# Moving 24 weight buffers by 64 bytes within each partition of on-chip memory: a spectral mix and two feed-forward layers on one core

## The chip, the cores and the metric

The kernel runs on one core of a Trainium2 chip. The metric is the device time of one execution in microseconds (us), taken as the median of several runs. A second number, the span, comes from one profiled execution: it runs from the first to the last instruction that the hardware profiler recorded.

## What is computed

The input is `x` of shape (4, 3072, 256). Three layers follow one another. The first is a Fourier transform along the sequence, a complex 256x256 product with `w_r` and `w_i`, a bias and a soft threshold, and the inverse transform. The second and third are:

```python
h = x @ w_in                               # (tokens, 256) @ (256, 2048): the first product
g = h * tanh(softplus(h))
x = g @ w_out                              # (tokens, 2048) @ (2048, 256): the second product

x_prev = x shifted by one token
xk = mu_k * x + (1 - mu_k) * x_prev
xr = mu_r * x + (1 - mu_r) * x_prev
k = relu(xk @ w_k)                         # 256 -> 1024
v = k * k @ w_v                            # 1024 -> 256
out = sigmoid(xr @ w_r2) * v               # w_r2 is moe2_w_r, 256 -> 256
```

All arrays are float32, and the three layers see 12288 tokens.

## The kernel before

**Precision.** A product in `part2` splits each operand into a high part `hi` (rounded to `F32R`, a float32 that TensorE takes in one pass) and the rest `lo`, and sums three matmuls: `wh*hi`, `wh*lo`, `wl*hi`. `mm(o, l, r, ...)` (L154) makes one MATMUL out of `r`, the operand that streams through the array (the moving one), with `l`, the operand that an LDWEIGHTS puts into the array first (the stationary one). Every MATMUL has its own LDWEIGHTS.

**Part 1** makes the transforms. `emit_F` multiplies lines of `a` (stationary) by the forward constants `fm` (moving), `emit_M` multiplies `xh`, `xl` (stationary) by the mixing weights `wmh`, `wml` (moving), and `emit_I` multiplies `yb` (stationary) by the inverse constants `im` (moving). `fm`, `im`, `a` and `yb` are plain float32.

**Part 2** takes the tokens in 24 blocks `j` of 512 and the hidden columns of the second layer in 16 chunks `c` of 128, so that a step `s` is a pair (j, c). Each step issues on TensorE, in this order: `emit_H(s)` (6 matmuls of 512 columns, tile `hps`), then whatever the table `PLAN` puts there of `emit_K` (6 of 512 columns, `kps`), `emit_V` (12 of 256 columns, `v`) and `emit_R` (12 of 256 columns, `zps`) for the third layer, and at last `emit_acc(s - 3)` (6 of 512 columns, `a`), the second product. ScalarE and VectorE turn `hps` into `gh`, `gl` and `kps` into `kh`, `kl` meanwhile.

**Where operands lie.** Pools take their place in a partition one behind the other, in the order in which they are opened. The small constants and `cst` end at byte 16576 of a partition, which is 192 modulo 256. Every tile from there on is a multiple of 256 bytes long, so that every operand begins at 192 modulo 256. One exception is there already: in `part2` a pool of 64 bytes stands ahead of `kk` (L819), so that `ka`, `kh`, `kl` and the tile `r` of pool `sg` begin at 0 modulo 256.

```python
            xk_p = pool(es, "xk", 1)
            pool(es, "gap", 1).tile([128, 16], F32, name="gap")
            kk_p = pool(es, "kk", 2)
```

The pool `mat` has 24 buffers of 2 KB. In part 1 they hold `fm` and `im`; later they are written again with `wo`, the weights of the second product (16 tiles, `wout_piece`, L487), and with `wkt`, the tiles of `w_k` (8 tiles, `fetch`, L510). The places of the operands of each product, modulo 256:

| product | rows named | stationary | moving | columns |
|---|---|---|---|---|
| first | hps<-yh,win / yl,win | `win` 192 | `yh`, `yl` 192 | 512 |
| second | a<-gh,wo / gl,wo | `wo` 192 | `gh`, `gl` 192 | 512 |
| w_k | kps<-xkh,wkt / xkl,wkt / b,wkt | `wkt` 192 | `xk` 192 | 512 |
| w_v | v<-b,kh / b,kl | `kh`, `kl` **0** | `wt["v"]` in `b` 192 | 256 |
| w_r2 | zps<-b | `xr` in `b` 192 | `wt["g"]` in `b` 192 | 256 |
| F, I (part 1) | xps<-fm,a / bps<-im,yb | `a`, `yb` 192 | `fm`, `im` 192 | 256 |
| mix (part 1) | yps<-wmh,xh and the like | `xh`, `xl` 192 | `wmh`, `wml` 192 | 512 |

Of the kernel before, what the change touches and what calls it, by code (L numbers as in the profile page):

```python
# [10 lines left out]
F32 = mybir.dt.float32  # L11
# [102 lines left out]
def tile_fft_mix_moe_channel_mix(  # L114
# [23 lines left out]
    def pool(stack, name, bufs, **kw):  # L138
        return stack.enter_context(tc.tile_pool(name=name, bufs=bufs, reuse_waits="tile", **kw))
# [21 lines left out]

    cst = pool(ctx, "cst", 1)
    big = pool(ctx, "big", 2)
    mat = pool(ctx, "mat", 24)
    g_p = pool(ctx, "g", 1)
    y_p = pool(ctx, "y", 1)
    yhl_p = pool(ctx, "yhl", 2)
# [900 lines left out]
```

## Time and profile before

| | |
|---|---|
| median of 3 runs | 1985.57 us (1985.16 to 1986.27) |
| the profiled execution, its own time | 1985.22 us |
| its span | 1983.2 us |
| PE (matmuls) busy | 1960.9 us, 10084 matmuls |
| PEld (weight loads) busy | 1687.4 us, 10084 loads |
| VectorE (DVE) / ScalarE (ACT) busy | 1143.1 us / 925.1 us |
| granted TensorE clock | 1.0 (the 2.4 GHz level) |

A matmul's duration in the profile is longer than the distance from its start to the next one's, since matmuls are pipelined. What counts for the time is the distance between starts.

### The profile page before, as it was taken

The page shows a single profiled execution, that of the slowest core. Times are in us where ns is not written, and L with a number is a line of the kernel's source. Part 1 is how long each engine was busy: PE and PEld are TensorE (multiplying, and loading weights), DVE is VectorE, ACT ScalarE, POOL GpSimd, SP SyncE. Part 2 cuts the span into 40 slices and gives each one's busy share as a digit, 9 for nine tenths or more (in the row PEclk, how much of TensorE's full clock was granted, in tenths as well). Part 3 has the DMA queues.
Part 4 walks back from the last instruction along what each step waited for, and adds up shares of the span by engine and source line. Part 5 has one row for each costly group of instructions (what it writes and reads, how often), then busy time and mean ns, then how long its engine had stood idle before and what let it go on. Part 6 is the DMA issues. An engine that isn't in the chain of part 4 may idle for free.

```text
span 1983.2 us, 25749 instructions
## 1 busy us (share of the span) xinstructions
PE 1960.9 (99%) x10084; PEld 1687.4 (85%) x10084; DVE 1143.1 (58%) x2183; ACT 925.1 (47%) x1525; POOL 13.5 (1%) x28
## 2 busy tenths in 40 slices
PE   6999999999999999999999999999999999999999
PEld 5888888888888888888888888888888888888888
DVE  8999986655654764465375445555444543444444
ACT  2423286344444544444444445444443544444455
POOL 0000000000000000000000000000000000000000
PEclk9999999999999999999999999999999999999999
DMA  9445276011011010101101001011000000000000
GB/s 278 151 136 170 71 246 202 34 33 64 22 33 54 22 46 9 54 22 33 54 22 54 1 22 54 8 31 38 22 1 22 22 11 11 22 22 1 22 11 22
DMA packets 104553, 106.66 MB, mean 54 GB/s; under 512 B 7016, under 2 KB 85488, under 8 KB 103408
## 3 DMA queue, kind: packets, MB, share of 16 engines
q1 hardware_dynamic: 104432, 105.02, 16.7%
q8 instruction: 79, 1.29, 0.3%
q14 instruction: 42, 0.34, 0.1%
HBM read 62.53 MB, written 42.47 MB: 53 GB/s over the span
## 4 chain that ended last, share of the span: by engine, by line
PE 97%; DMA 1%; DVE 1%; ACT 1%; issue 0%; SPq 0%; DVEq 0%; ACTq 0%
PE a L155 26%; PE hps L155 26%; PE v L155 14%; PE kps L155 13%; PE yps L155 7%; PE bps L155 4%; PE xps L155 4%; PE zps L155 3%; DMA a<-in_x_dram 0%; DMA w_dr<-wp 0%; DMA wraw<-in_w_r_dram 0%; DMA im<-in_inv_dram 0%; ACT sg L152 0%; SPq L266 0%; DVE q L149 0%
## 5 line engine op out<-in xcount | busy, mean ns | idle before, releaser
L864 DVE CAST gh<-u 128x512 fp32r<-128x512 f32 x384 | 163.4, 425 | 685.1 <-PE a L155 594.3
L155 PE MATMUL a<-gh,wo 128*128 128x512 f32 x1536 | 536.7, 390 | 0.0
L155 PE MATMUL hps<-yh,win 128*128 128x512 f32 x1536 | 534.7, 389 | 0.0
L152 ACT ACTIVATE u<-hps 128x512 f32<-128x512 f32 x384 | 229.7, 598 | 483.1 <-PE hps L155 428.5
L155 PEld LDWEIGHTS hps<-yh,win 128*128 128x128 f32 x1536 | 288.4, 188 | 60.4
L155 PEld LDWEIGHTS a<-gh,wo 128*128 128x128 f32 x1536 | 288.6, 188 | 57.8
L155 PE MATMUL a<-gl,wo 128*128 128x512 f32 x768 | 300.1, 391 | 0.0
L155 PE MATMUL hps<-yl,win 128*128 128x512 f32 x768 | 298.8, 389 | 0.0
L155 PE MATMUL v<-b,kh 128*128 128x256 f32 x1536 | 279.8, 281 | 0.0
L146 DVE TENSOR_TENSOR gl<-u,gh 128x512 fp32r<-128x512 f32 x384 | 263.9, 687 | 3.6
L155 PEld LDWEIGHTS v<-b,kh 128*128 128x128 f32 x1536 | 249.6, 189 | 14.3
L155 PE MATMUL v<-b,kl 128*128 128x256 f32 x768 | 215.8, 281 | 0.0
L152 ACT ACTIVATE ka<-kps 128x512 f32<-128x512 f32 x192 | 114.8, 598 | 211.0 <-PE kps L155 210.9
L155 PEld LDWEIGHTS hps<-yl,win 128*128 128x128 f32 x768 | 144.2, 188 | 29.8
L155 PEld LDWEIGHTS a<-gl,wo 128*128 128x128 f32 x768 | 144.7, 188 | 25.7
L146 DVE TENSOR_TENSOR kl<-ka,kh 128x512 fp32r<-128x512 f32 x192 | 132.9, 692 | 44.0 <-ACT ka L152 29.4
L155 PE MATMUL kps<-xkl,wkt 128*128 128x512 f32 x384 | 150.7, 392 | 0.0
L155 PEld LDWEIGHTS v<-b,kl 128*128 128x128 f32 x768 | 144.2, 188 | 0.0
L155 PE MATMUL kps<-b,wkt 128*128 128x512 f32 x384 | 134.5, 391 | 0.0
L155 PE MATMUL kps<-xkh,wkt 128*128 128x512 f32 x384 | 134.0, 391 | 0.0
L152 ACT ACTIVATE ka<-ka 128x512 f32<-128x512 f32 x192 | 121.8, 634 | 6.1
L152 ACT ACTIVATE kh<-ka 128x512 fp32r<-128x512 f32 x192 | 121.6, 633 | 6.1
(80 smaller groups left out, 2069.8 us busy)
## 6 DMA issues: line engine op xcount, KB each, us to landing
b_dr<-bs SPq DMA_DIRECT2D x48, 256.0 KB, 2.2
g<-b_dr SPq DMA_DIRECT2D x8, 1536.0 KB, 6.7
y<-y_dr SPq DMA_DIRECT2D x48, 256.0 KB, 3.1
out_dram<-r SPq DMA_DIRECT2D x48, 256.0 KB, 2.2
y_dr<-g SPq DMA_DIRECT2D x80, 64.0 KB, 1.7
w_dr<-wp SPq DMA_DIRECT2D x9, 512.0 KB, 5.8
a<-in_x_dram SPq DMA_DIRECT2D x8, 512.0 KB, 6.2
y_dr<-g SPq DMA_DIRECT2D x32, 128.0 KB, 1.9
```

The lines of the kernel that those rows point to most:

```text
L146: V.tensor_tensor(out=o, in0=a, in1=b, op=op)
L152: S.activation(out=o, in_=i, func=f, **kw)
L155: T.matmul(out=o, lhsT=l, rhs=r, start=start, stop=stop, **kw)
L864: return [lambda: V.tensor_copy(hi, u), lambda: tt(lo, u, hi.bitcast(F32), SUB)]
```

## The change

Two unused pools are opened around `mat`. The first is 64 bytes long and moves `mat` by 64 bytes; the second is 192 bytes long, so that everything behind it moves by 256 bytes in all and keeps its place modulo 256.

```diff
     cst = pool(ctx, "cst", 1)
     big = pool(ctx, "big", 2)
+
+    pool(ctx, "gap1", 1).tile([128, 16], F32, name="gap1")
     mat = pool(ctx, "mat", 24)
+    pool(ctx, "gap2", 1).tile([128, 48], F32, name="gap2")
     g_p = pool(ctx, "g", 1)
```

`fm`, `im`, `wo` and `wkt` now begin at 0 modulo 256; every other operand stays at 192, and `kk` and `sg` stay at 0. Each engine issues the same instructions in the same order as before.

## Rows read from the trace of the kernel before

**Rows 1.** The page: busy time of each engine, and the granted clock.

```profile
PE 1960.9 (99%) x10084; PEld 1687.4 (85%) x10084; DVE 1143.1 (58%) x2183; ACT 925.1 (47%) x1525; POOL 13.5 (1%) x28
...
PEclk9999999999999999999999999999999999999999
```

**Rows 2.** Waits of PE: all there are.

```profile
PE xps L155 <- DVE g L146: 17.6, 2, 16.2
PE yps L155 <- ACT zl L628: 0.5, 1, 0.5
PE bps L155 <- DVE yb L149: 0.2, 1, 0.2
```

**Rows 3.** Groups of instructions: matmuls by product (count, busy us, mean ns).

```profile
L155 PE MATMUL a<-gh,wo 128*128 128x512 f32 x1536 | 536.7, 390 | 0.0
L155 PE MATMUL hps<-yh,win 128*128 128x512 f32 x1536 | 534.7, 389 | 0.0
L155 PE MATMUL a<-gl,wo 128*128 128x512 f32 x768 | 300.1, 391 | 0.0
L155 PE MATMUL hps<-yl,win 128*128 128x512 f32 x768 | 298.8, 389 | 0.0
L155 PE MATMUL v<-b,kh 128*128 128x256 f32 x1536 | 279.8, 281 | 0.0
...
L155 PE MATMUL kps<-xkl,wkt 128*128 128x512 f32 x384 | 150.7, 392 | 0.0
...
L155 PE MATMUL kps<-b,wkt 128*128 128x512 f32 x384 | 134.5, 391 | 0.0
L155 PE MATMUL kps<-xkh,wkt 128*128 128x512 f32 x384 | 134.0, 391 | 0.0
...
L155 PE MATMUL bps<-im,yb 128*128 128x256 f32 x384 | 90.6, 379 | 0.2 <-DVE yb L149 0.2
...
L155 PE MATMUL xps<-fm,a 128*128 128x256 f32 (+1 forms) x352 | 80.6, 372 | 0.0
L155 PE MATMUL zps<-b 128*128 128x256 f32 x576 | 76.6, 283 | 0.0
```

**Rows 4.** Timeline of PE, an R group, then second product, H, V (start, us).

```profile
984.44 1.60 PE L155 MATMUL zps<-b 128*128 128x256 f32 x12
985.88 0.40 PE L155 MATMUL a<-gh,wo 128*128 128x512 f32 x1
...
987.26 0.39 PE L155 MATMUL hps<-yh,win 128*128 128x512 f32 x1
...
988.62 0.40 PE L155 MATMUL v<-b,kh 128*128 128x256 f32 x2
...
990.04 0.40 PE L155 MATMUL kps<-b,wkt 128*128 128x512 f32 x1
```

**Rows 5.** Timeline of PEld around the change from H to V.

```profile
1022.49 0.19 PEld L155 LDWEIGHTS hps<-yh,win 128*128 128x128 f32 x1
1022.72 0.41 PEld L155 LDWEIGHTS v<-b,kh 128*128 128x128 f32 x2
```

**Rows 6.** Groups at 1022.72 us: the last two matmuls of H ahead of V.

```profile
L155 PE MATMUL hps<-yl,win 128*128 128x512 f32 x1 | 0.4, 389 | 0.0
L155 PE MATMUL hps<-yh,win 128*128 128x512 f32 x1 | 0.4, 388 | 0.0
```

**Rows 7.** Groups at 984.22 us: the last two matmuls of H ahead of R.

```profile
L155 PE MATMUL hps<-yh,win 128*128 128x512 f32 x1 | 0.4, 389 | 0.0
```

**Rows 8.** Groups from 985.87 to 987.25 us: the second product behind an R group.

```profile
L155 PE MATMUL a<-gh,wo 128*128 128x512 f32 x4 | 1.4, 392 | 0.0
L155 PE MATMUL a<-gl,wo 128*128 128x512 f32 x2 | 0.8, 396 | 0.0
```

**Rows 9.** Timeline of PE in part 1: an I and an F group.

```profile
57.65 1.89 PE L155 MATMUL bps<-im,yb 128*128 128x256 f32 x8
59.37 1.89 PE L155 MATMUL xps<-fm,a 128*128 128x256 f32 x8
```

## The prediction

> **What bounds the kernel now.** I first read the busy shares and the clock: TensorE is busy for 99% of the span, and its granted clock stays at the upper level, 2.4 GHz [rows 1]. Then the waits: all waits of its matmuls come to 18.3 us, of which 17.6 are two waits of the first transforms for `g` [rows 2]. So nothing that another engine does sets the time; it is the sum of the distances between matmul starts. The third view is the groups by product [rows 3]. What a reader is to compare there is the mean duration of matmuls of one shape. A duration is not the distance between starts, but the two move together: 12 `zps` matmuls of 283 ns begin within 985.88 - 984.44 = 1.44 us, 120 ns apart, and 12 `v` matmuls of 281 ns within 990.04 - 988.62 = 1.42 us, 118 ns apart [rows 4]. Both times the duration is the distance plus 163 ns. So a mean in rows 3 that falls by 1 ns is 1 ns of span for each matmul.
>
> **What the change touches.** It neither adds nor removes an instruction, and no engine's order moves. What is new is one relation: for `a` (1536 + 768 matmuls) and `kps` (3 x 384), 3456 matmuls together [rows 3], the weights that are loaded begin at 0 modulo 256 while the operand that streams begins at 192. Before, both began at 192. The weights of one matmul are loaded while the one before it streams: the load for the first `v` begins at 1022.72, the start of the last `hps` [rows 5, 6]. So if the two reads get in each other's way, the place of one against the other could matter. Three comparisons within before bear on it.
>
> 1. *Matmuls of 256 columns, one behind the other.* `v` is the only product whose weights (`kh`, `kl`) lie at 0 while its moving operand lies at 192. `zps` has the same shape, the same high-high-low order, and both at 192. `v` takes 281 ns, `zps` 283 [rows 3]. If the place is the reason, it is worth 2 ns a matmul.
> 2. *One matmul of 512 columns with a shifted load under it.* The last `hps` ahead of a V group streams from 192 while weights at 0 are loaded: 388 ns [rows 6]. The last `hps` ahead of an R group has weights at 192 under it: 389 ns [rows 7]. All else about the two is alike. This is just the situation in which the change puts each `a` and `kps`, and it is worth 1 ns.
> 3. *Matmuls of 512 columns right behind 256-column groups.* They are slow whatever the place: after R, where everything lies at 192, the six of the second product take 4 x 392 + 2 x 396 = 2360 ns instead of 6 x 389 = 2334, 26 ns more [rows 8]. By the means, these slow groups cost 1536 x 1 + 768 x 2 (`a`) + 384 x 3 + 768 x 2 (`kps`) = 5.8 us in all against 389 [rows 3]. That `kps` and `a` are dearer than `hps` is thus a matter of what stands ahead of them, for rows of undisturbed groups are at 389 too. I leave these 5.8 us as they are; the bounds are that they go (-5.8) and that all groups become so (rival 3).
>
> **The sum.** A load at 0 comes under one matmul for each of the 3456, six for each group of six (the first under the last matmul of the group ahead). I take the 1 ns of comparison 2, since it has the same 512 columns and the same two places: 3456 x 1 ns = 3.5 us less. With the price of comparison 1 it is 3456 x 2 = 6.9 us less; these matmuls have 512 columns and those of comparison 1 have 256, so I take the nearer row and keep 6.9 as a bound. Durations are whole nanoseconds, so that the 1 ns itself may be anything from a half to one and a half: 1.7 to 5.2 us.
>
> The rest I cost at nothing:
> - *`fm` and `im` as moving operands.* `bps` and `xps` are float32 matmuls; eight `bps` records begin within 59.37 - 57.65 = 1.72 us, 215 ns apart [rows 9], for 256 columns, which is nearly double the 118 to 120 ns of `v` and `zps`. Columns are read half as fast, and no row here has the two operands at different places. With the 2 ns of comparison 1 in either direction, the 384 + 352 records [rows 3] are worth 1.5 us at most.
> - *Writes into `mat`* (loads of `fm`, `im`, `wkt`, and the decoding of `wo`) are work of DMA, ScalarE and VectorE, which TensorE does not wait for [rows 2]; if that cover were gone, those 17.6 us are the only place where it would show, and the tiles there (`g`, `a`) do not move modulo 256.
> - *Everything behind the second gap* moves by 256 bytes. `kps<-b` and `kps<-xkh` take 391 ns each [rows 3] though `b` begins at 69824 and `xkh` at 192960, which differ by 256 modulo 512: a shift by 256 bytes shows nothing.
>
> The profiled execution took 1985.22 us with a span of 1983.2; 3.5 less is 1981.7 and a span of 1979.7. The median of the runs stands 0.35 us higher, so the forecast for the median is 1985.57 - 3.5 = **1982.1 us**, 0.18% less. A measurement of this kernel can tell about 0.2%, 4.0 us, from no change, so that this counts as the same by a little.
>
> **The rivals.**
> 1. *The place does not matter at all* and the time stays at 1985.6. Then `v` differs from `zps` for another reason (other weights, another accumulator), and the 388 ns of rows 6 come from the kind of matmul that follows. Against it: the matmul ahead of `zps`, also of 256 columns, has 389 [rows 7]. For it speaks a rule. The Trainium skill says, on the page "TensorE: Matmul & The Clock Gate", section "Step-by-step: what each phase is for", that TensorE has two independent read ports, so that loading the next weights takes no read bandwidth from the running matmul; by that rule no place could change anything, and the sum would be 0. The 281 against 283 ns do not fit it, but they do not disprove it either.
> 2. *The dear end of the gain.* The steady pattern in which every load is shifted is worth what `v` shows: 2 ns on 3456, 1985.6 - 6.9 = 1978.7; if the slow groups of 26 ns go as well, another 5.8, 1972.9. For it: `v` is the only long run of shifted loads. Against it: in `v` loads and matmuls follow each other twice as densely.
> 3. *Slower.* The distance of a load from the stream decides, and 64 bytes can also bring the worse distance. Rows 8 show that the same two operands at the same places can cost 26 ns in six when they start in another rhythm, so the 389 ns is no ceiling. If the shift makes this the standing rhythm of `a` and `kps`, the groups that do not pay yet begin to: 3456 / 6 = 576 groups, of which 5.8 / 0.026 = 223 pay already, leaves 353 x 26 ns = 9.2 us, 1994.8. It decides from the point where a matmul with a shifted load under it stands above 389 ns inside a group and not only at its edge; rows 6 show one matmul at the edge, and nothing about the next. Half of it, if only one of the two products falls into that rhythm, is 1990.
>
> **How the numbers follow.** The forecast (1.7 to 5.2 us less) has 0.40, no effect 0.20, the larger gain 0.20, slower 0.17, and 0.03 is left for a much larger gain (the reads no longer meet at all). Faster by more than 0.2% are the larger gains and the upper quarter of the forecast: 0.2 + 0.03 + 0.10 = 0.33. Slower by more than 0.2% are rival 3 and a price of `fm` and `im` that comes on top of it or of no effect: 0.20. The rest, 0.47, is the same. The range takes in the 2 ns with half of the slow groups gone, 6.9 + 2.9 = 9.8 below (1975.8), and most of rival 3, 7.4 above (1993.0): outside lie the rest of rival 2 and the upper half of rival 3, less than 2 in 10. The forecast's own range is 1980.4 to 1983.9.
>
> **What would show it.** Right: in the groups by product, `a<-gh` goes from 390 to 389, `a<-gl` from 391 to 390, `kps` down by 1, while `hps`, `v` and `zps` keep 389, 281 and 283; an undisturbed `a` matmul stands at 388; `bps` keeps 379. Rival 1: all means stay. Rival 2: undisturbed `a` and `kps` at 387, or no step up behind `v` and `zps`. Rival 3: `a` and `kps` at 392 and above also where `hps` or `kps` stands ahead. The forecast is wrong in its reason if the time moves and these means do not, above all if `xps`, `bps` or a wait has moved instead.

## The result, and the profile after

The changed kernel takes 2004.85 us (median of 5 runs, 2004.69 to 2005.22) against 1985.57: a ratio of 1.0097 with a 95% interval of 1.0086 to 1.0108. It is 19.3 us slower, where 3.5 us less had been forecast, and it lies outside the range, whose upper end was 1993.0. The span of the profiled execution went from 1983.2 to 2002.7 us, 19.5 more.

The page of the changed kernel shows the same bound as before [rows 1]:

```profile
PE 1980.9 (99%) x10084; PEld 1682.8 (84%) x10084; DVE 1143.4 (57%) x2183; ACT 923.6 (46%) x1525; POOL 13.5 (1%) x28
...
PEclk9999999999999999999999999999999999999999
```

TensorE is busy 20.0 us longer, the loads are not (1687.4 to 1682.8), and the clock stays at the 2.4 GHz level. The waits of PE, in the order us, times, longest, do not grow either [rows 2]:

```profile
PE xps L155 <- DVE g L146: 17.0, 2, 15.6
PE bps L155 <- DVE yb L149: 0.3, 1, 0.3
PE yps L155 <- ACT zl L631: 0.3, 1, 0.3
```

So TensorE waits no longer than before, and it is matmuls themselves that take longer. The groups by product (count, busy us, mean ns) tell which [rows 3]:

```profile
L155 PE MATMUL a<-gh,wo 128*128 128x512 f32 x1536 | 544.4, 395 | 0.0
L155 PE MATMUL hps<-yh,win 128*128 128x512 f32 x1536 | 538.8, 392 | 0.0
L155 PE MATMUL a<-gl,wo 128*128 128x512 f32 x768 | 303.9, 396 | 0.0
L155 PE MATMUL hps<-yl,win 128*128 128x512 f32 x768 | 301.9, 393 | 0.0
L155 PE MATMUL v<-b,kh 128*128 128x256 f32 x1536 | 275.6, 279 | 0.0
L155 PE MATMUL v<-b,kl 128*128 128x256 f32 x768 | 213.6, 278 | 0.0
L155 PE MATMUL kps<-xkl,wkt 128*128 128x512 f32 x384 | 152.2, 396 | 0.1
L155 PE MATMUL kps<-b,wkt 128*128 128x512 f32 x384 | 136.0, 395 | 0.0
L155 PE MATMUL kps<-xkh,wkt 128*128 128x512 f32 x384 | 135.5, 395 | 0.0
L155 PE MATMUL bps<-im,yb 128*128 128x256 f32 x384 | 90.7, 379 | 0.4 <-DVE yb L149 0.3
L155 PE MATMUL xps<-fm,a 128*128 128x256 f32 (+1 forms) x352 | 80.6, 372 | 0.0
L155 PE MATMUL zps<-b 128*128 128x256 f32 x576 | 76.5, 283 | 0.0
```

Mean against mean: `a` 5 ns on 2304 matmuls is 11.5 us; `kps` 4 ns on 1152 is 4.6; `hps`, whose operands did not change their places, 3 ns on 1536 and 4 on 768, 7.7; `v`, unchanged as well, 2 ns less on 1536 and 3 less on 768 (281 before for both), -5.4. The sum is 18.4 of the 19.5 us; means are in whole nanoseconds. Part 1 with its `fm` and `im` did not move (379 and 372 as before), nor did `zps`. The line of `v<-b,kl` before, which [rows 3] leaves out:

```profile
L155 PE MATMUL v<-b,kl 128*128 128x256 f32 x768 | 215.8, 281 | 0.0
```

The timeline of PE shows the same in the groups of six and twelve. Each line is the first matmul of a group (start in us):

```profile
1002.49 0.39 PE L155 MATMUL kps<-b,wkt 128*128 128x512 f32 x1
...
1003.89 0.40 PE L155 MATMUL a<-gh,wo 128*128 128x512 f32 x1
...
1005.29 0.39 PE L155 MATMUL hps<-yh,win 128*128 128x512 f32 x1
...
1006.68 0.41 PE L155 MATMUL v<-b,kh 128*128 128x256 f32 x2
...
1008.06 0.39 PE L155 MATMUL a<-gh,wo 128*128 128x512 f32 x1
...
1009.46 0.39 PE L155 MATMUL hps<-yh,win 128*128 128x512 f32 x1
...
1010.83 0.40 PE L155 MATMUL a<-gh,wo 128*128 128x512 f32 x1
```

`kps` and `a` take 1.40 us each, `hps` behind them 1.39, and `v` 1.38. Before, six undisturbed matmuls took 1.36 us (from 987.26 to 988.62 in [rows 4]), and `v` 1.42. The `a` behind `v` also takes 1.40, but a group behind matmuls of 256 columns was slow already, 1.38 in [rows 4], and so grows by less; the `hps` behind it takes only 1.37.

### The profile page after: what moved, and what is told of

The parts are those of the page before. It is cut to its first block, busy times and chain, and to the rows that moved or that the text cites. A ratio compares the mean times of both kernels' runs of the same rounds, so it can differ in the third digit from the quotient of the medians.

```text
span 2002.7 us, 25749 instructions
## 1 busy us (share of the span) xinstructions
PE 1980.9 (99%) x10084; PEld 1682.8 (84%) x10084; DVE 1143.4 (57%) x2183; ACT 923.6 (46%) x1525; POOL 13.5 (1%) x28
## 4 chain that ended last, share of the span: by engine, by line
PE 94%; DVE 4%; DMA 1%; ACT 0%; SPq 0%; issue 0%; DVEq 0%
PE a L155 27%; PE hps L155 26%; PE kps L155 13%; PE v L155 13%; PE yps L155 5%; PE zps L155 3%; PE bps L155 3%; PE xps L155 3%; DVE a L146 1%; DVE a L149 1%; DVE yb L149 0%; DVE q L149 0%; DMA w_dr<-wp 0%; DVE xl L146 0%; DMA a<-in_x_dram 0%; DMA im<-in_inv_dram 0%
## 5 line engine op out<-in xcount | busy, mean ns | idle before, releaser
L155 PE MATMUL a<-gh,wo 128*128 128x512 f32 x1536 | 544.4, 395 | 0.0
L155 PE MATMUL v<-b,kh 128*128 128x256 f32 x1536 | 275.6, 279 | 0.0
```

Source lines behind the costliest of these rows:

```text
L155: T.matmul(out=o, lhsT=l, rhs=r, start=start, stop=stop, **kw)
```

## The experiments

Eleven kernels ran. They issue the same instructions in the same order; only places differ. Times are medians, each beside runs of the kernel before on the same chip (1985.6). "Place" is the place modulo 256. Streams begin at 192 unless they are moved: weights at 0 then lie 64 bytes behind them (at a higher address), weights at 128 lie 64 bytes ahead.

### Moving everything by 256 bytes (mat256)

```diff
+    pool(ctx, "gap1", 1).tile([128, 64], F32, name="gap1")
     mat = pool(ctx, "mat", 24)
```

> Everything from the pool mat on lies 256 bytes further, so that all places modulo 256 are those of the kernel before. Theory A (what costs is the relation of a load to the stream modulo 256): within 1.5 us of 1985.6, a and kps at 390 to 392 ns, hps 389. Theory B (what costs is that mat was moved at all, or its distance from big in bytes): 1995 to 2005, a at 395 ns and hps at 392.

Measured: 1985.48 us, ratio 1.0 (0.9989 to 1.0011), `a` at 390 and 391 ns, `hps` at 389, as before. Theory B falls: that `mat` moved, and that it lies 256 bytes further from `big`, costs nothing. What costs must be a place within 256 bytes.

### 128 bytes, and 64 bytes the other way (mat128, mat192)

```diff
+    pool(ctx, "gap1", 1).tile([128, 32], F32, name="gap1")
     mat = pool(ctx, "mat", 24)
+    pool(ctx, "gap2", 1).tile([128, 32], F32, name="gap2")
```

This is mat128; in mat192 the two are 48 and 16 floats long.

> mat lies 128 bytes off (64 modulo 256), the rest keeps its place modulo 256. Theory A: not the time of before, and not that of 64 bytes either: if the cost grows with the distance, 2010 to 2025 (a above 395 ns); if 64 bytes is a bad place and 128 is away from it, 1975 to 1995. Theory B: 2005 within 2 us, as with 64 bytes.

> The change with the other sign: wo and wkt at 128, 64 bytes ahead of the streams instead of 64 behind. Theory F without a sign (any mismatch throws the rhythm off): 1998 to 2008, undisturbed a groups near 1398 ns. If the sign decides also for 512 columns, as it did for what follows v (kk128): a groups at or under 1360 ns and 1978 to 1990.

Measured: 2005.93 us (1.0103, 1.0073 to 1.0132) with weights 128 bytes behind the streams, `a` at 395 and 396 ns; 1991.98 us (1.0034, 1.0023 to 1.0046) with weights 64 bytes ahead of them. For mat128 theory A missed on both sides, and the time is the one that theory B gave, which mat256 excludes. The total is near that of 64 bytes, but its parts are not the same: `a` pays as much, `hps<-yl` (390 ns) and `kps` (393 to 395) pay less, and `v` gives hardly anything back (280 and 281). For mat192 both cases missed the time. The sign matters, but for matmuls of 512 columns no distance tried (64 bytes either way, 128) beats none. Part of the 6.4 us of mat192 lies in part 1, whose `fm` and `im` moved too: its `yps` matmuls rose by 2 to 4 ns (from 429, 381 and 380 to 433, 383 and 382). In mat192 a `kps` group takes 1.38 us and an `a` group behind it 1.37 (timeline of PE):

```profile
997.85 0.39 PE L155 MATMUL kps<-b,wkt 128*128 128x512 f32 x1
...
999.23 0.39 PE L155 MATMUL a<-gh,wo 128*128 128x512 f32 x1
...
1000.60 0.39 PE L155 MATMUL hps<-yh,win 128*128 128x512 f32 x1
```

### One of the two products alone (wo_only, wk_only)

`mat` becomes two pools of 16 and 8 buffers; `wo` later lies in the one and `wkt` in the other, and only one of them is moved (shown for `wo`).

```diff
-    mat = pool(ctx, "mat", 24)
+    pool(ctx, "gapa", 1).tile([128, 16], F32, name="gapa")
+    mat = pool(ctx, "mat", 16)
+    pool(ctx, "gapb", 1).tile([128, 48], F32, name="gapb")
+    mk = pool(ctx, "mk", 8)
...
-                    fm[ORD[i]] = mat.tile([128, 2, 256], F32, tag="m", name="fm")
+                    fm[ORD[i]] = (mat if len(fm) + len(im) < 16 else mk).tile([128, 2, 256], F32, tag="m", name="fm")
...
-            wt["k", c] = mat.tile([128, 2, 2, 128], F32R, tag="m", name="wkt")
+            wt["k", c] = mk.tile([128, 2, 2, 128], F32R, tag="m", name="wkt")
```

> Two pools in place of mat, 16 buffers that later hold wo and 8 that later hold wkt; only the first pool lies 64 bytes off. Theory A: about two thirds of the 19.3 us, 1998 (1995 to 2001), kps behind H at 389 to 390 ns, and hps slow only behind a. If the loss came from kps or from fm and im alone: below 1990 or unchanged at 2005.

> Only the pool that holds wkt lies 64 bytes off. Theory F (a mismatched load throws the rhythm of loads and streams off, and the groups behind it need about five 512-column matmuls to come back): kps 1395 to 1400 ns a group also behind H (1360 before), and the second product behind it, whose operands match, 24 to 28 ns a group dearer; hps back at 389; 1993 to 1997. Theory A2 (only the mismatched matmuls pay): kps 4 to 6 us dearer in all, the second product unchanged, 1990 to 1992.

Measured: 2000.83 us for `wo` alone (1.0077, 1.0048 to 1.0106), 1994.73 for `wkt` alone (1.0046, 1.0030 to 1.0062), both inside what was expected (1995 to 2001, and 1993 to 1997 by theory F). The timeline of PE with `wkt` alone moved:

```profile
996.65 0.39 PE L155 MATMUL hps<-yh,win 128*128 128x512 f32 x1
...
998.01 0.40 PE L155 MATMUL kps<-b,wkt 128*128 128x512 f32 x1
...
999.41 0.39 PE L155 MATMUL a<-gh,wo 128*128 128x512 f32 x1
...
1000.80 0.39 PE L155 MATMUL hps<-yh,win 128*128 128x512 f32 x1
...
1002.16 0.40 PE L155 MATMUL v<-b,kh 128*128 128x256 f32 x2
```

The moved product takes 1.40 us. The second product behind it, whose loads and streams all begin at 192, takes 1.39 instead of 1.36, and the `hps` behind that is back at 1.36. With `wo` alone it is the other way round: `hps` behind an `a` takes 1.39, then `kps` 1.36, then the next `a` 1.40 and the `hps` behind it 1.39 again:

```profile
999.54 0.39 PE L155 MATMUL hps<-yh,win 128*128 128x512 f32 x1
...
1000.93 0.39 PE L155 MATMUL kps<-b,wkt 128*128 128x512 f32 x1
...
1002.29 0.40 PE L155 MATMUL a<-gh,wo 128*128 128x512 f32 x1
...
1003.69 0.39 PE L155 MATMUL hps<-yh,win 128*128 128x512 f32 x1
...
1005.08 0.41 PE L155 MATMUL v<-b,kh 128*128 128x256 f32 x2
...
1006.46 0.39 PE L155 MATMUL a<-gh,wo 128*128 128x512 f32 x1
```

So a disturbed group also makes the next group of 512 columns dearer, by some 30 ns, and then it is over: theory F, and not A2. Here `v` takes 1.38 us, as in the changed kernel, and with `wkt` alone it keeps 281 ns: here it gains where the `hps` ahead of it is still disturbed at its last matmul. (An `hps` behind an `a` that stands itself behind `v` or `zps` pays only some 10 ns and has come back by then.)

wo_only also has the situation of the prediction's comparison 2 in the product that the change touches: the last `kps` ahead of a moved `a`, and then the six of `a` (groups from 1002.29 to 1003.67 us):

```profile
L155 PE MATMUL a<-gh,wo 128*128 128x512 f32 x4 | 1.4, 395 | 0.0
L155 PE MATMUL a<-gl,wo 128*128 128x512 f32 x2 | 0.8, 396 | 0.0
L155 PE MATMUL kps<-b,wkt 128*128 128x512 f32 x1 | 0.4, 388 | 0.0
```

The `kps`, under which the first moved weights are loaded, gains its 1 ns against 389. The six behind it stand 6 to 7 ns above it.

### The same place for both operands of the second product (after_gh64)

The changed kernel, with `gh` and `gl` moved too:

```diff
+            pool(es, "gap3", 1).tile([128, 16], F32, name="gap3")
             gh_p = pool(es, "gh", G_BUFS)
+            pool(es, "gap4", 1).tile([128, 48], F32, name="gap4")
```

> The changed kernel, and gh, gl (the streamed operand of the second product) also 64 bytes further, so that both operands of the second product begin at 0 modulo 256; kps stays apart. Theory A: the part of the second product (2304 of 3456 matmuls) goes, 2004.9 - 12.9 = 1992, undisturbed a at 389 ns. Theory C (weights at 0 modulo 256 are bad in themselves, whatever streams): 2005, a at 395 ns.

Measured: 2004.23 us (1.0094, 1.0065 to 1.0124). The groups by product:

```profile
L155 PE MATMUL a<-gh,wo 128*128 128x512 f32 x1536 | 542.3, 394 | 0.0
L155 PE MATMUL a<-gl,wo 128*128 128x512 f32 x768 | 299.2, 390 | 0.0
L155 PE MATMUL v<-b,kh 128*128 128x256 f32 x1536 | 279.5, 281 | 0.0
L155 PE MATMUL v<-b,kl 128*128 128x256 f32 x768 | 215.7, 281 | 0.0
```

The time is theory C's, and theory A's 1992 is missed. Yet theory C falls too: between the changed kernel and this one the weights of the second product stay at 0 and only its streams move, and `a` gets cheaper, `a<-gh` from 395 to 394 ns and `a<-gl` from 396 to 390, 6.1 us in all. So the relation of the two counts, not the place 0. The time stays because `v` has lost its gain (279 and 278 back to 281), 5.4 us. That the time agrees with theory C is thus two changes that cancel. The timeline of PE:

```profile
1002.05 0.40 PE L155 MATMUL kps<-b,wkt 128*128 128x512 f32 x1
...
1003.45 0.39 PE L155 MATMUL a<-gh,wo 128*128 128x512 f32 x1
...
1004.83 0.39 PE L155 MATMUL hps<-yh,win 128*128 128x512 f32 x1
...
1006.22 0.40 PE L155 MATMUL v<-b,kh 128*128 128x256 f32 x2
```

`a` takes 1.38, less than the 1.40 of the changed kernel, yet not 1.36. Inside the group loads and streams now agree, but at both its ends one load does not: weights at 0 come in while the group ahead streams from 192, and `win` at 192 while the last `gh` streams from 0. `hps` behind it takes 1.38 to 1.39; `v` behind this `hps` gains nothing, unlike in wo_only. `a` and `hps` also take 1.38 us each in steps that hold no `kps`, so that this is not carried over from there. What is left is the switch of places between neighbouring products, two in every step, which theory A in its first form had left out. No run has such a switch alone, so that this part is argued and not shown.

### Another product in the same position (big64)

```diff
+    pool(ctx, "gap1", 1).tile([128, 16], F32, name="gap1")
     big = pool(ctx, "big", 2)
+    pool(ctx, "gap2", 1).tile([128, 48], F32, name="gap2")
```

> The pool big lies 64 bytes off and everything else keeps its place modulo 256: now win is loaded from 0 while yh, yl stream from 192, wt v and kh both lie at 0, and of kps every second block streams from 0 over weights from 192. Theory F: the first product takes what the second took, 1398 ns a group instead of 1360, 384 x 38 ns = 14.6 us, the second product behind it pays 24 ns a group = 9.2 us, v goes to 120 ns (5.2 us): 2010 to 2018. Theory C (weights from the pool mat are special): 1990 or less.

Measured: 2011.73 us (1.0131, 1.0111 to 1.0151), inside the 2010 to 2018 of theory F. The groups by product, three lines of them:

```profile
L155 PE MATMUL hps<-yh,win 128*128 128x512 f32 x1536 | 543.9, 395 | 0.0
L155 PE MATMUL a<-gh,wo 128*128 128x512 f32 x1536 | 540.9, 393 | 0.0
L155 PE MATMUL v<-b,kh 128*128 128x256 f32 x1536 | 282.3, 282 | 0.0
```

`hps` now stands at the 395 ns that `a` had in the changed kernel, with its weights at 0 under a stream from 192, and `a`, all at 192, pays behind it. Nothing about the pool `mat` or about `wo` is special. By the means `hps` pays the 14.6 us that were expected, but `a` only 4.6 of 9.2 and `v` 2.3 of 5.2, while `kps`, which had no price, pays some 2.7: that the total came out is in part luck. For `v` the run shows the relation once more: `kh` and `kl` lie at 0 as in the kernel before, the stream has moved to 0 as well, and `v` goes from 281 to 282 ns, as it does with all operands at 192 (kk192, next).

### Is it the place that makes `v` faster than `zps`? (kk192)

The 64 bytes ahead of `kk`, which the kernel before has, are taken out:

```diff
-            pool(es, "gap", 1).tile([128, 16], F32, name="gap")
             kk_p = pool(es, "kk", 2)
```

> The kernel before without its 64-byte pool ahead of kk: kh, kl begin at 192 like everything else. Theory D (the place makes v faster than zps): v from 281 to 283 ns, 120 ns apart, 2304 x 2.3 ns = 5.2 us more, 1990.8. Theory E (v differs from zps for another reason): v keeps 281 and the time stays within 1 us of 1985.6.

Measured: 1989.47 us, 1.0020 (1.0010 to 1.0029). The groups by product:

```profile
L155 PE MATMUL v<-b,kh 128*128 128x256 f32 x1536 | 283.1, 282 | 0.0
L155 PE MATMUL v<-b,kl 128*128 128x256 f32 x768 | 217.3, 283 | 0.0
```

`v` takes what `zps` takes: theory D, and comparison 1 of the prediction was read rightly. The size is 3.9 us, where 2 ns on 2304 matmuls are 4.6. The last `hps` ahead of `v` is back at 389 ns too, from 388: comparison 2 also read an effect of the place.

### Other places for `kh` and `kl` (kk128, kk64, kk160)

The pool ahead of `kk` is 192, 128 or 224 bytes long instead of 64, so that `kh`, `kl` begin at 128, 64 or 160.

```diff
-            pool(es, "gap", 1).tile([128, 16], F32, name="gap")
+            pool(es, "gap", 1).tile([128, 48], F32, name="gap")
```

This is kk128; the pool has 32 floats in kk64 and 56 in kk160.

> The kernel before with 192 instead of 64 bytes ahead of kk: kh, kl at 128, 64 bytes ahead of everything else instead of 64 behind. Theory F with a sign: another v period than 117.7 ns, either 113 to 116 (1977 to 1982) or back at 120 (1991). If only being apart counts: 117.7 ns and 1985.6 within 1 us.

> kh, kl at 64, 128 bytes off the rest. Theory F: v stays between 113 and 120 ns, whichever the distance, and only v and the group behind it move: 1981 to 1990; a and kps behind H keep 1360 ns a group.

> kh, kl at 160, 32 bytes ahead of the rest (64 bytes ahead gave 1982.0). If the gain of 64 bytes ahead is the crossing of a boundary of 64 bytes: nothing here against all at 192, 1989.5; if it grows with the distance: between 1982 and 1989.5; if any distance ahead serves: 1982.

| `kh`, `kl` against the rest | time us | ratio to before (95%) | `v<-b,kh` mean ns | 12 `v`, us | `hps<-yh` mean ns | `kps<-xkl` mean ns |
|---|---|---|---|---|---|---|
| 64 ahead (kk128) | 1982.03 | 0.9982 (0.9972 to 0.9992) | 279 | 1.41 | 389 | 390 |
| 32 ahead (kk160) | 1984.31 | 0.9993 (0.9982 to 1.0005) | 280 | 1.40 | 390 | 392 |
| 64 behind (before) | 1985.57 | | 281 | 1.41 | 389 | 392 |
| none (kk192) | 1989.47 | 1.0020 (1.0010 to 1.0029) | 282 | 1.43 | 389 | 392 |
| 128 (kk64) | 1995.25 | 1.0048 (1.0028 to 1.0068) | 283 | 1.45 | 390 | 393 |

"12 `v`" is the distance from the start of a `v` group behind `hps` to the start of the next group, on the mean.

Weights 64 bytes ahead of the stream give a faster kernel than 64 behind or no distance. For kk64 the expected 1981 to 1990, and `v` at or under 120 ns apart, were wrong: it is slower than with no distance, and 1.45 us for twelve `v` are 121 ns. For kk160 the time falls into the middle case, but not by its reason, and it is not told apart from before: at 32 bytes ahead `v` itself is faster than at 64, while the group behind `v` gains nothing and the last `hps` ahead of it takes 396 ns instead of 388. So the gain does not simply grow with the distance. In kk128 `v` keeps its distance, as the third case had it, and the time falls all the same. (The mean of 279 ns misleads here: 2 ns on 2304 matmuls would be more than the whole gain of 3.5 us, and twelve `v` take what they took before.) What gains is the group behind (timeline of PE):

```profile
997.34 0.40 PE L155 MATMUL v<-b,kh 128*128 128x256 f32 x2
...
998.75 0.40 PE L155 MATMUL a<-gh,wo 128*128 128x512 f32 x1
...
1000.12 0.39 PE L155 MATMUL hps<-yh,win 128*128 128x512 f32 x1
```

`v` takes 1.41 us, as on the mean before, but the `a` behind it 1.37, where such a group behind 256-column matmuls took 1.38 before [rows 4, 8]. The means of `a<-gl` and `kps<-xkl` fell accordingly, from 391 to 390 and from 392 to 390 ns.

## Why the prediction was wrong

**What bounds the kernel** was right: no wait changed, and the time is the sum of the distances between matmul starts. **Comparison 1** was right in its cause (kk192). That a shift by 256 bytes shows nothing was right (mat256), and so were the zeros for `fm`, `im` and for the writes into `mat`: 379 and 372 ns stayed. That 1 ns of a mean is 1 ns of span for each matmul held for the changed kernel (18.4 of 19.5 us), but not for `v` in kk128.

**The step that failed is comparison 2 and the sum made from it**: "This is just the situation in which the change puts each `a` and `kps`, and it is worth 1 ns." It priced a mismatched load by the one matmul under which it runs, the last `hps` ahead of `v` [rows 6, 7]. That matmul was the first of its kind, behind five undisturbed ones, and what came behind it were matmuls of 256 columns, which have another rhythm. The 1 ns itself is there (389 in kk192, and 388 for the last `kps` in wo_only), but it belongs to that one matmul: wk_only and wo_only show that the price falls on the matmuls behind. When every load of a group of 512 columns is mismatched, the group takes 1.40 us instead of 1.36, about 7 ns more a matmul and not 1 less; the group behind pays up to 30 ns more even if its own operands agree. The sum was therefore wrong in sign and also short of a product: `hps` is not touched by the change and pays 7.7 us. A second product that was not touched, `v`, gives 5.4 us back.

**Rival 3** named the right mechanism, with 0.17: the 64 bytes bring a worse standing rhythm. It is not the one of rows 8, though, and its price was too small. It took 26 ns a group from the groups behind 256-column matmuls and let it stand in 353 more groups, 9.2 us. Measured are 40 ns a group (1.40 against 1.36) where the group was undisturbed before, 16.1 us in `a` and `kps` together, and the 7.7 us that are carried over into `hps`, less the 5.4 that `v` gives back. Its test ("`a` and `kps` at 392 and above also where `hps` or `kps` stands ahead") is met: 395 and 396.

**Rival 1** falls. The Trainium skill's sentence on two independent read ports (page "TensorE: Matmul & The Clock Gate", section "Step-by-step: what each phase is for") would have the running matmul lose nothing to the next load wherever the two lie. The measurement decides against it for this case: with the same instructions, places alone give 1985.5 (mat256), 1992.0 (mat192) or 2004.9 us. **Rival 2** falls for 512 columns: neither 64 bytes either way nor 128 was faster than none.

**Left open:** which part of the memory the two reads share, why a disturbance lasts for a group, and what decides between the two rhythms of `v`. In the changed kernel, in wo_only and in after_gh64, a `v` group behind `hps` takes 1.37 to 1.38 us where the last `hps` stands at 391 ns or more, and 1.41 where it is back at 388; that fits `v` gaining nothing in after_gh64, where `hps` has come back by its last matmul. In mat128 it does not hold: `v` takes 1.41 or 1.42 us behind an `hps` that ends at 392, and 1.37 behind one that ends at 398. The runs show that the place of a load against the stream modulo 256 decides, that the sign matters, and that a disturbance outlasts its cause by one group of 512 columns. They do not show the structure behind it; distances other than 32 (ahead, for `kh` and `kl` alone), 64 and 128 bytes were not tried.

## What to carry to other kernels

Where TensorE is the bound, as here, look at places too. Matmuls of 512 columns with a weight load each were fastest with loaded and streamed operands at one place modulo 256, throughout all products that follow each other. The one product of 256 columns that was tried, `v`, gained with weights 64 bytes off the stream either way or 32 ahead, and lost at 128; with 64 ahead the group behind gained too. A comparison that lies at the edge of a group prices the edge only: before such a price is multiplied by thousands, look at the matmuls behind, and at the product that follows.

## What the runs showed that had not been expected

- Places alone, with not one instruction changed, span 1982.0 us (kk128) to 2011.7 (big64), 1.5%.
- A disturbance is carried into the next product: +30 ns for a group whose own operands agree (1.39 against 1.36 us in wk_only), and none in the group of 512 columns after it.
- A time can agree with a theory by cancelling: in after_gh64 `a` gained 6.1 us and `v` lost 5.4, and the total looked as if nothing had happened.
- The same 12 `v` matmuls, with their operands at the same places, take 1.38 us in wo_only and 1.41 to 1.42 before, by what stands ahead of them.
